# A pair's weighted sums and memory transposes issued as one run of matmuls, with the short pair's last blocks padded to 128 rows

## The chip, the cores and the metric

The kernel runs on one core of a Trainium2 chip. The metric is the device time of one execution in microseconds (us), the median of several runs. Beside those runs stands one execution taken by the hardware profiler, which records every instruction of every engine. The engines are PE (TensorE: matmuls; their weight loads are listed apart as PEld), DVE (VectorE), ACT (ScalarE), POOL (GpSimd) and SP (SyncE, which issues the DMAs). Each engine works through its own queue in order, and semaphores let one engine wait for another.

## The reference: what is computed

Attention over 4 batches, 8 heads, 576 positions and 64 dimensions, mixed with a read of a memory matrix, and then two feed-forward layers over the 2304 tokens:

```python
scores = scale * np.matmul(q, k.transpose(0, 1, 3, 2))      # causal mask, softmax -> a
local = np.matmul(a, v)
q_p = phi(q)                                                # where(x > 0, x, exp(x) - 1) + 1
mem_out = einsum('bhsd,bhde->bhse', q_p, M_prev) / (einsum('bhsd,bhd->bhs', q_p, z_prev)[..., None] + 1e-6)
x = g * mem_out + (1 - g) * local                           # g = sigmoid(beta), one value a head
h = x @ w_in;  x2 = (h * sigmoid(1.702 h)) @ w_out          # 512 -> 2048 -> 512
h = x2 @ w_in2;  out = (h * clip(h + 3, 0, 6) / 6) @ w_out2
```

## The kernel before, in words

**Tiles and pairs.** The tokens are cut into six tiles of 384. Tiles 0, 1, 3 and 4 are the first 384 positions of one batch; tiles 2 and 5 hold the last 192 positions of two batches each. Attention works on pairs of heads: a *long pair* has 384 query rows and 384 keys, a *short pair* has 192 query rows (positions 384 to 575) and 576 keys. There are 16 long pairs, four to each of tiles 0, 1, 3 and 4, and 16 short ones, eight to each of tiles 2 and 5.

**Feed-forward.** For each of two layers and six tiles, 16 units follow one another (`moe`, line 271). A unit makes `h` in four quarters of three matmuls (lines 305 to 307), passes it through a gate (ACT, DVE, ACT, POOL: lines 257 to 268), and adds to four `y` with twelve matmuls (lines 285 to 287). Weights and activations are split into a high and a low part, hence three matmuls where one would stand. The weights arrive raw and are converted by a chain of seven or eight instructions a piece (`conv_w`, lines 188 to 230, on DVE, POOL and ACT), 32 pieces a layer.

**Attention of the next tile runs between the feed-forward matmuls of this one.** The attention of tile 0 is a prologue with no feed-forward beside it. For a pair, `scores` makes the scores `s` and their softmax `p`; `turn` transposes `p` on PE into PSUM (`t`, `t4a`, `t4b`), and ACT or DVE copies it to SBUF (`pt`, and `t4` for the short pair's last 64 keys by 64 rows); `mem_read` (line 626) multiplies phi(q) with the memory (`mem`), and DVE divides and weighs it (`mw`, `mo`, lines 646 to 653); `weigh` (line 663) adds into one PSUM bank `o` the weighted sums `v.T pt`, for the two heads in the two column halves of the array (64 output rows each), and then the transposes of `mo` through the identity. ACT copies `o` to `x`, and `split_x` (line 247) makes of `x` the `xs` that the next tile's `h` reads.

**Sizes on the array.** The profile writes a matmul's rows*columns of the array: `128*128` for feed-forward, transposes, most scores and the memory read, `128*64` for the weighted sums, `64*64` for the `t4` block and the short pair's last scores, `64*128` for the scores of pairs read unsplit. An fp32 matmul shows as two instructions.

**What sets the order.** The generators yield, and `pump` (line 800) interleaves their pieces with the feed-forward by a rate (PG0, PG1). A scheduler that plans with a model of the engines' times then fixes each engine's order, with two restraints: a feed-forward `h` quarter is issued only after the attention matmul recorded `SLACK` pieces earlier (`behind`, line 303), and named DMAs and weight steps stay in program order. `need` (line 363) only makes sure that the instructions of a chain have been written before their reader is; it is no wait on the chip.

**After the last attention.** The pool of the attention's tiles is closed and its memory given to `x2p`, in which the first six raw pieces of the second layer's weights and the second layer's first activations are loaded. These loads therefore stand behind the last pair's last matmul, and the second layer's conversions behind the loads.

Of the kernel before, what the change touches and what calls it, by code (L numbers as in the profile page):

```python
# [24 lines left out]
KQ = 100  # L25
CR = 3.75
OFF = 3
# [9 lines left out]
T4B = 1  # L37
# [73 lines left out]
def attention_moe_kernel(ctx: ExitStack, tc: tile.TileContext, qk0, sk0, sk1, vm0, vm1, bb, w1, w2, out):  # L111
# [76 lines left out]
    def conv_w():  # L188

        key = layer, f, a = w_jobs[w_at[1]]  # L190
# [160 lines left out]

    def at_transpose(*args):
        on_pe[:] = [PE.transpose(*args).ins]  # L353

    def attention(ap):
        qk, vm, pp, pt, phi, mo, raw, sp = {}, {}, {}, {}, {}, {}, {}, {}
        gens = {}
        norms, cut = [0, 0], set()

# [184 lines left out]
        def evac(jobs):  # L544

            yield
            for e, out, in_ in jobs:
                if e is ACT:
                    ACT.copy(out=out, in_=in_)
                else:  # L550
                    DVE.tensor_copy(out=out, in_=in_)

        def turn(i):
            ti, si, b, g, p, _ = pairs[i]
            if g == 0:
                pt[i] = []
                for a in range(2):
# [4 lines left out]
                    for jj in range(2):  # L562
# [4 lines left out]
                        start(("t", i, a, jj), evac([((ACT, DVE)[EV0[jj]], t[:, jj * 384:(jj + 1) * 384], ps[:, 0:384])]))  # L567
                        yield
            else:
                t4 = ap.tile([64, 2, 64], F32, tag="t4", bufs=T4B, name="t4")  # L570
                pt[i] = []
                for a in range(2):
# [4 lines left out]
                    for j in range(4):  # L577
# [3 lines left out]
                        evac([((ACT, DVE)[EV1[a]], t[:, :, 0:128], ps.rearrange("p (j c) -> p j c", j=4))]),  # L581
                    )
                    yield
                pt[i].append(t4)
# [3 lines left out]
                for j in range(3):  # L588
# [8 lines left out]
                        [((ACT, DVE)[EV1[2 + a]], pt[i][a][:, 0:3, 128:192], v[:, :, a]) for a in range(2)]  # L597
                        + [(DVE, pt[i][a][:, 3, 128:192], ps2[:, a * 64:(a + 1) * 64]) for a in range(2)]
                        + [(DVE, t4, ps2[0:64, 128:256].rearrange("p (a c) -> p a c", a=2))]
# [5 lines left out]
        def rows(g):  # L605
            return ((0, 128), (128, 128), (256, 128)) if g == 0 else ((0, 128), (128, 64))
# [19 lines left out]
        def mem_read(i):  # L626
# [7 lines left out]
            for k, (r0, nr) in enumerate(rr):  # L634
                at_matmul(a[0:nr, k * 130:(k + 1) * 130], lhsT=e[:, r0:r0 + nr], rhs=m, start=True, stop=True)
# [4 lines left out]
            def scale():  # L640
                yield
                v = a[:, 0:390].rearrange("p (k c) -> p k c", k=3)
                grp = ((0, 3, 128),) if g == 0 else ((0, 1, 128), (1, 2, 64))
                for k0, k1, nr in grp:
                    wk = w[0:nr, k0:k1]
                    DVE.tensor_scalar(out=wk, in0=v[0:nr, k0:k1, 128:130], scalar1=1e-6, scalar2=None, op0=ALU.add)
                    DVE.reciprocal(out=wk, in_=wk)
                    DVE.tensor_tensor(
                        out=wk, in0=wk, in1=gall[0:nr, None, 2 * p:2 * p + 2].to_broadcast([nr, k1 - k0, 2]), op=ALU.mult
# [277 lines left out]
```

## Time and profile before

| | us |
|---|---|
| median of 3 runs (1100.32 to 1103.64) | 1102.02 |
| the profiled execution's own time | 1097.73 |
| its span, first to last instruction | 1095.9 |
| PE busy in the span | 1052.0 (96%) |
| DVE, ACT, POOL busy | 570.7, 539.1, 472.1 |

The granted clock is the part of TensorE's full rate (2.4 GHz) that it got in a stretch; its lower level is half (1.2 GHz). "Busy" counts an instruction from its start to its modelled end, so for PE the distance from one start to the next is the better price. An engine's idle time costs only where something later waits for it, and the stretches of this kernel differ in which engine that is.

### The profile page before, as it was taken

The numbers are of one execution on the slowest core, as the hardware profiler recorded it, in microseconds if no ns is written. First come the engines' busy times: TensorE is split into PE (matmuls) and PEld (weight loads), VectorE is DVE, ScalarE is ACT, GpSimd is POOL, SyncE is SP. The second block draws the span as 40 slices with busy tenths as digits, with TensorE's granted clock in tenths as the row PEclk, the third lists the DMA queues.
The fourth block names the chain that finished last, engine by engine and source line by source line (L and its number), as shares of the span: only waits on it lengthen the run. The fifth ranks groups of instructions, "written<-read, shape, count | busy, mean of one in ns | idle before, by whom it ended". The sixth has DMA issues, their size and how long they took to land.

```text
span 1095.9 us, 17060 instructions
## 1 busy us (share of the span) xinstructions
PE 1052.0 (96%) x6153; PEld 958.1 (87%) x6153; DVE 570.7 (52%) x1511; ACT 539.1 (49%) x1225; POOL 472.1 (43%) x526
## 2 busy tenths in 40 slices
PE   7988779999999999999999998998999999999998
PEld 5566667788889999889888997998999999999998
DVE  7899999635766564435445588884111121111210
ACT  6766665544555555435443566765233232332422
POOL 5688867544444435444543344543222222222221
PEclk9989989999999999999999998999999999999999
DMA  7542322212231212212120585101000010000000
GB/s 245 202 184 101 121 82 63 73 58 74 82 106 54 63 40 82 69 48 73 44 63 25 204 294 176 57 1 44 15 29 30 1 59 1 30 29 1 30 1 29
DMA packets 32627, 81.77 MB, mean 75 GB/s; under 512 B 3744, under 2 KB 12960, under 8 KB 32544
## 3 DMA queue, kind: packets, MB, share of 16 engines
q1 hardware_dynamic: 32544, 80.69, 21.9%
q8 instruction: 48, 0.79, 0.3%
q14 instruction: 35, 0.29, 0.1%
HBM read 71.24 MB, written 9.44 MB: 74 GB/s over the span
## 4 chain that ended last, share of the span: by engine, by line
PE 76%; DVE 11%; issue 6%; POOL 5%; ACT 1%; DMA 1%; SPq 0%; POOLq 0%; ACTq 0%; DVEq 0%
PE h L305 10%; PE h L307 10%; PE h L306 10%; PE y L287 10%; PE y L286 10%; PE y L285 10%; PE o L350 6%; PE s L350 5%; PE t L353 3%; POOL r L209 2%; POOL g L268 2%; DVE r L205 2%; DVE r L200 2%; PE mem L350 1%; DVE s L391 1%
## 5 line engine op out<-in xcount | busy, mean ns | idle before, releaser
L268 POOL TENSOR_TENSOR g<-t,g 128x384 fp32r<-128x384 f32 x176 | 183.5, 1043 | 407.7 <-ACT g L266 380.9
L305 PE MATMUL h<-xs,w 128*128 128x384 f32 x768 | 266.9, 348 | 19.8 <-DVE t L259 12.3
L306 PE MATMUL h<-xs,w 128*128 128x384 f32 x768 | 261.1, 340 | 0.3 <-DVE w L228 0.3
L307 PE MATMUL h<-xs,w 128*128 128x384 f32 x768 | 261.1, 340 | 0.3 <-DVE xs L251 0.2
L285 PE MATMUL y<-g,w 128*128 128x384 f32 x768 | 259.1, 338 | 0.6 <-ACT g L266 0.5
L286 PE MATMUL y<-g,w 128*128 128x384 f32 x768 | 257.4, 336 | 0.0
L287 PE MATMUL y<-g,w 128*128 128x384 f32 x768 | 241.4, 339 | 3.1 <-DVE g L268 2.9
L263 DVE SCALAR_TENSOR_TENSOR t<-t,h 128x384 f32<-128x384 f32 x96 | 53.1, 553 | 272.1 <-ACT t L261 272.1
L305 PEld LDWEIGHTS h<-xs,w 128*128 128x128 f32 x768 | 147.2, 192 | 30.3 <-DVE t L259 16.7
L266 ACT CAST g<-t 128x384 fp32r<-128x384 f32 x192 | 98.5, 513 | 111.6 <-DVE t L259 56.8
L287 PEld LDWEIGHTS y<-g,w 128*128 128x128 f32 x768 | 141.4, 188 | 9.1 <-DVE g L268 3.9
L307 PEld LDWEIGHTS h<-xs,w 128*128 128x128 f32 x768 | 146.8, 191 | 1.6 <-DVE xs L251 1.1
L306 PEld LDWEIGHTS h<-xs,w 128*128 128x128 f32 x768 | 147.2, 192 | 1.1 <-DVE w L228 0.6
L285 PEld LDWEIGHTS y<-g,w 128*128 128x128 f32 x768 | 144.7, 188 | 3.2 <-issue 1.0
L286 PEld LDWEIGHTS y<-g,w 128*128 128x128 f32 x768 | 144.5, 188 | 0.3
L261 ACT ACTIVATE t<-h,three 128x384 f32<-128x384 f32 x96 | 55.6, 579 | 169.6 <-PE h L307 169.6
L404 POOL TENSOR_SCALAR p<-p,st,omg 128x128 f32<-128x128 f32 (+2 forms) x128 | 93.4, 737 | 84.3 <-DVE st L400 58.7
L391 DVE CUSTOM_DVE_ANT_0 s<-s,mask 128x128 f32<-128x128 f32 (+2 forms) x144 | 73.8, 519 | 74.7 <-PE s L350 73.5
L396 ACT ACTIVATE p<-s,st 128x128 f32<-128x128 f32 (+3 forms) x160 | 82.9, 524 | 25.7 <-DVE st L391 23.3
L259 DVE SCALAR_TENSOR_TENSOR t<-t,h 128x384 f32<-128x384 f32 x96 | 52.7, 549 | 62.1 <-ACT t L257 59.0
L257 ACT ACTIVATE t<-h 128x384 f32<-128x384 f32 x96 | 47.0, 490 | 61.6 <-PE h L307 54.4
L209 POOL TENSOR_SCALAR r<-r 128x512 f32<-128x512 f32 x64 | 57.1, 895 | 30.5 <-DVE r L205 22.4
(86 smaller groups left out, 1348.2 us busy)
## 6 DMA issues: line engine op xcount, KB each, us to landing
r<-in_w_dram SPq DMA_DIRECT2D x64, 512.0 KB, 5.0
raw<-in_sk_dram SPq DMA_DIRECT2D x50, 384.0 KB, 3.2
vm<-in_vm_dram SPq DMA_DIRECT2D x16, 386.0 KB, 3.0
x2d<-yo SPq DMA_DIRECT2D x24, 192.0 KB, 2.0
xr<-x2d SPq DMA_DIRECT2D x24, 192.0 KB, 3.1
out_dram<-yo SPq DMA_DIRECT2D x24, 192.0 KB, 1.9
vm<-in_vm_dram SPq DMA_DIRECT2D x16, 258.0 KB, 2.8
qk<-in_qk_dram SPq DMA_DIRECT2D x7, 384.0 KB, 3.8
```

The costliest lines, as they stand in the source:

```text
L266: gated["ACT"].append(ACT.copy(out=g[:, 0], in_=t).ins)
L268: d = (DVE, POOL)[GLE[ti if layer == 0 else -1]].tensor_tensor(out=g[:, 1], in0=t, in1=f32(g[:, 0]), op=ALU.subtract)
L285: PE.matmul(ys[d], lhsT=w[:, 0, o:o + 128], rhs=g[:, 0], start=(f == 0), stop=False)
L286: PE.matmul(ys[d], lhsT=w[:, 1, o:o + 128], rhs=g[:, 0], start=False, stop=False)
L287: PE.matmul(ys[d], lhsT=w[:, 0, o:o + 128], rhs=g[:, 1], start=False, stop=(f == NF - 1))
L305: PE.matmul(h, lhsT=w[:, 0, c:c + 128], rhs=x[:, 0], start=(kk == 0), stop=False)
L306: PE.matmul(h, lhsT=w[:, 1, c:c + 128], rhs=x[:, 0], start=False, stop=False)
L307: PE.matmul(h, lhsT=w[:, 0, c:c + 128], rhs=x[:, 1], start=False, stop=(kk == KD - 1))
L350: on_pe[:] = [PE.matmul(out, **args).ins]
L391: DVE.tensor_tensor_reduce(out=o, in0=o, in1=m, scale=-SCALE, scalar=init, op0=ALU.add, op1=ALU.min, accum_out=out)
L396: ACT.activation(out=dst, in_=o, func=AF.Exp, scale=-1.0, bias=m, accum_out=s)
L404: (DVE, POOL)[e[norms[0] % len(e)]].tensor_scalar(out=dst, in0=dst, scalar1=s, scalar2=w, op0=ALU.mult, op1=ALU.mult)
```

## The change

Five things are edited. `weigh` first asks for everything that the pair needs, and issues its weighted sums and memory transposes through `in_a_run`: the first matmul waits for the last copy of `pt`/`t4` and the last `mo` on each engine, and the others are chained to it in order, with no yield between them. For short pairs, the `t4` block becomes one tile of 128 rows whose lower 64 rows are zero, set once. The memory read's second block takes rows 64 to 191 instead of 128 to 191, so that it too has 128 columns; the gates `gall` grow to four slices, the last of them zero for the 64 rows that are there twice, so one group of small DVE instructions serves both blocks and the second memory transpose is 128 by 128. A weight piece is started only when the piece four before it has been written out in full. The rates follow the smaller number of yields: KQ 100 to 90, 48 to 44, 76 to 67.

```diff
-KQ = 100
+KQ = 90
...
-T4B = 1
+GW = (0, 2)
...
     def conv_w():
 
-        key = layer, f, a = w_jobs[w_at[1]]
+        n = w_at[1]
+        key = layer, f, a = w_jobs[n]
+        if n >= 4 and w_jobs[n - 4] in w_gen:
+            chains.finish(w_gen[w_jobs[n - 4]])
...
+    def after(ins, deps):
+
+        for dep in deps:
+            tc.add_manual_dep(
+                ins, dep.name, mybir.DependencyInfo(mybir.DependencyClass.Sync, mybir.DependencyReason.DATA),
+                reason="one run of matmuls",
+            )
+
+    def in_a_run(deps):
+
+        run = []
+
+        def mm(out, **args):
+            ins = PE.matmul(out, **args).ins
+            if run:
+                tc.add_manual_dep(
+                    ins, run[-1].name,
+                    mybir.DependencyInfo(mybir.DependencyClass.NoSync, mybir.DependencyReason.DATA),
+                    reason="one run of matmuls",
+                )
+            else:
+                after(ins, deps)
+            run.append(ins)
+            on_pe[:] = [ins]
+
+        return mm
...
+        t4 = ap.tile([128, 2, 64], F32, tag="t4", bufs=1, name="t4")
+        POOL.memset(t4, 0.0)
...
-                        + [(DVE, t4, ps2[0:64, 128:256].rearrange("p (a c) -> p a c", a=2))]
+                        + [(DVE, t4[0:64], ps2[0:64, 128:256].rearrange("p (a c) -> p a c", a=2))]
...
-            return ((0, 128), (128, 128), (256, 128)) if g == 0 else ((0, 128), (128, 64))
+            return (0, 128, 256) if g == 0 else (0, N1 - 128)
...
-            for k, (r0, nr) in enumerate(rr):
-                at_matmul(a[0:nr, k * 130:(k + 1) * 130], lhsT=e[:, r0:r0 + nr], rhs=m, start=True, stop=True)
+            nb = len(rr)
+            for k, r0 in enumerate(rr):
+                at_matmul(a[:, k * 130:(k + 1) * 130], lhsT=e[:, r0:r0 + 128], rhs=m, start=True, stop=True)
...
+                DVE.tensor_tensor(out=wk, in0=wk, in1=gall[:, GW[g]:GW[g] + nb, 2 * p:2 * p + 2], op=ALU.mult)
...
+            need(("t", i, 0, 0), ("t", i, 0, 1), ("t", i, 1, 0), ("t", i, 1, 1), ("m", i))
             o = bank("o")
+            mm = in_a_run(list(made.pop(i).values()))
...
             if g == 0:
-                need(("t", i, 0, 0), ("t", i, 1, 0))
-                av(0, lambda a: t[a][:, 0:384], 0, 384, 128, True)
-                yield
-                need(("t", i, 0, 1), ("t", i, 1, 1))
-                av(1, lambda a: t[a][:, 384:640], 128, 384, 128, False)
-                av(2, lambda a: t[a][:, 640:768], 256, 384, 128, False)
+                av(0, lambda a: t[a][:, 0:384], 0, 384, True)
+                av(1, lambda a: t[a][:, 384:640], 128, 384, False)
+                av(2, lambda a: t[a][:, 640:768], 256, 384, False)
             else:
-                need(("t", i, 0, 0), ("t", i, 1, 0), ("t", i, 0, 1))
                 for j in range(4):
-                    av(j, lambda a: t[a][:, j], 0, N1, 128, j == 0)
-                    if j == 1:
-                        yield
-                av(4, lambda a: t[2][:, a], 128, N1, 64, False)
-            need(("m", i))
+                    av(j, lambda a: t[a][:, j], 0, N1, j == 0)
+                av(4, lambda a: t4[:, a], 128, N1, False)
...
+            POOL.memset(gall[0:64, 3], 0.0)
+            ACT.copy(out=gall[:, 1:3], in_=gall[:, 0:1].to_broadcast([128, 2, H]))
+            ACT.copy(out=gall[64:128, 3], in_=gall[64:128, 0])
...
-                pump((qi - OFF) / (PG0 * 128 / 48 if TILES[ti + 1][0][1] == 0 else PG1 * 128 / 76))
+                pump((qi - OFF) / (PG0 * 128 / 44 if TILES[ti + 1][0][1] == 0 else PG1 * 128 / 67))
```

The order of PE's instructions in the prologue, around the weighted sums of the third pair (a long one); `o<-pt,vm` are the weighted sums, `o<-ident,mo` the memory transposes, `t` the transposes of `p`, `s_...` the scores. First before:

```order
L353 MATMUL t<-ident,p 128x128 x5
L350 MATMUL o<-pt,vm 64x384
L350 MATMUL s_496<-qk 128x128
L350 MATMUL s_496<-qk 128x256
L350 MATMUL s_516<-qk 128x384
L353 MATMUL t<-ident,p 128x128 x3
L350 MATMUL s_546<-qk 128x128
L350 MATMUL s_546<-qk 128x256
L350 MATMUL o<-pt,vm 64x384
L353 MATMUL t<-ident,p 128x128 x3
L350 MATMUL o<-pt,vm 64x256
L353 MATMUL t<-ident,p 128x128 x2
```

The order of PE at the same place of the change, the third pair's weighted sums again:

```order
L353 MATMUL s_501<-qk 128x128
L353 MATMUL s_501<-qk 128x256
L383 MATMUL t<-ident,p 128x128 x6
L368 MATMUL o<-pt,vm 64x384 x2
L368 MATMUL o<-pt,vm 64x256 x2
L368 MATMUL o<-pt,vm 64x128 x2
L368 MATMUL o<-ident,mo 128x128 x3
L353 MATMUL s_571<-qk 128x384
```

What stood in four pieces, one head's matmul apart from the other's, stands in one.

PE's order in the feed-forward of tile 4, around a short pair of tile 5 (`o<-t_...` is the `t4` block); before:

```order
L287 MATMUL y_5424<-g,w_931 128x384
L350 MATMUL o<-pt,vm 64x192 x4
L350 MATMUL s_5932<-sp 128x512 x2
L350 MATMUL o<-pt,vm 64x192 x4
L350 MATMUL o<-t_5742,vm 64x64 x2
L350 MATMUL o<-ident,mo 128x128
L350 MATMUL o<-ident,mo 128x64
L353 MATMUL t<-ident,p 128x128 x4
```

PE's order around a short pair at that place in the change:

```order
L290 MATMUL y_5392<-g,w_1041 128x384
L368 MATMUL o<-pt,vm 64x192 x8
L368 MATMUL o<-t_111,vm 64x64 x2
L368 MATMUL o<-ident,mo 128x128 x2
L353 MATMUL s_5898<-sp 128x512 x2
L383 MATMUL t<-ident,p 128x128 x4
```

The scores have moved behind the run, and both memory transposes have one shape. (The order names a matmul by its output rows and columns of data; the padded `t4` block has the same 64x64 here, on 128 rows of the array.)

The last pair of all on PE, before: the end of its run, and the start of tile 4's last unit (weights `w_1766`; `xs_5275` is tile 4's):

```order
L350 MATMUL o<-t_6353,vm 64x64 x2
L287 MATMUL y_5423<-g,w_1688 128x384
L285 MATMUL y_5424<-g,w_1688 128x384
L286 MATMUL y_5424<-g,w_1688 128x384
L350 MATMUL o<-ident,mo 128x128
L350 MATMUL o<-ident,mo 128x64
L287 MATMUL y_5424<-g,w_1688 128x384
L305 MATMUL h<-xs_5275,w_1766 128x384
```

The last pair of all on PE in the change; `xs_6490`, `xs_6496`, `xs_6502` are the first three quarters of tile 5, and `w_1791` is tile 4's last unit:

```order
L310 MATMUL h<-xs_6502,w_322 128x384
L288 MATMUL y_5389<-g,w_1791 128x384
L289 MATMUL y_5389<-g,w_1791 128x384
L288 MATMUL y_5390<-g,w_1791 128x384
L289 MATMUL y_5390<-g,w_1791 128x384
L288 MATMUL y_5391<-g,w_1791 128x384
L289 MATMUL y_5391<-g,w_1791 128x384
L288 MATMUL y_5392<-g,w_1791 128x384
L289 MATMUL y_5392<-g,w_1791 128x384
L368 MATMUL o<-pt,vm 64x192 x8
L368 MATMUL o<-t_111,vm 64x64 x2
L368 MATMUL o<-ident,mo 128x128 x2
```

Before, the run ends ahead of tile 4's last unit; now it stands behind that unit's 12 `h` and the 12 `y` of the unit before it, nine `h` of tile 5 and eight `y` of the last unit, 41 feed-forward matmuls later.

DVE's order there in the change (`mo` is the last pair's scaled memory, `xs_6508` tile 5's fourth quarter, `t<-t,h` a gate, `r_6537` and `r_6539` the second layer's first raw pieces):

```order
L682 TENSOR_TENSOR mo<-mem,mw 128x128 x2
L254 TENSOR_TENSOR xs_6508<-x_5891,xs_6508 128x384
L262 SCALAR_TENSOR_TENSOR t<-t,h 128x384
L203 TENSOR_SCALAR r_6537<-r_6537 128x512
L262 SCALAR_TENSOR_TENSOR t<-t,h 128x384 x2
L203 TENSOR_SCALAR r_6539<-r_6539 128x512
```

The first conversion stands behind the gate of a tile-5 unit, as it did before, but that gate now needs a quarter which the last run makes.

## Rows read from the trace of the kernel before

**Rows 1.** Five stretches (--windows): length, busy (instructions) by engine, clock, DMA share, GB/s.

```profile
0.00:56.00 56.00, 47.74 (x236) 29.08 (x236) 45.37 (x190) 39.04 (x118) 33.59 (x53) 0.97 0.64 227
56.00:197.00 141.00, 117.67 (x633) 97.85 (x632) 138.83 (x297) 89.81 (x196) 110.41 (x104) 0.92 0.31 106
197.00:611.50 414.50, 414.15 (x2587) 362.43 (x2588) 217.84 (x763) 207.44 (x536) 178.55 (x225) 1.00 0.21 65
611.50:753.20 141.70, 133.28 (x748) 130.22 (x746) 113.26 (x164) 94.98 (x173) 66.99 (x64) 0.98 0.39 134
753.20:1095.90 342.70, 339.19 (x1954) 338.56 (x1954) 55.37 (x101) 107.86 (x205) 82.60 (x82) 1.00 0.07 24
```

**Rows 2.** PE's timeline: a short pair cut by scores; columns start, busy us.

```profile
545.26 0.87 PE L350 MATMUL o<-pt,vm 128*64 128x192 f32 x8
546.06 0.73 PE L350 MATMUL s<-sp 128*128 128x512 f32 x2
546.72 0.87 PE L350 MATMUL o<-pt,vm 128*64 128x192 f32 x8
547.52 0.33 PE L350 MATMUL o<-t,vm 64*64 64x64 f32 x4
547.79 0.53 PE L350 MATMUL o<-ident,mo 128*128 128x128 f32 x2
548.25 0.66 PE L353 MATMUL t<-ident,p 128*128 128x128 f32 x4
```

**Rows 3.** PE's timeline: a short pair's sums not cut.

```profile
592.09 1.52 PE L350 MATMUL o<-pt,vm 128*64 128x192 f32 x16
593.54 0.33 PE L350 MATMUL o<-t,vm 64*64 64x64 f32 x4
```

**Rows 4.** PE's timeline: a memory read of a short and of a long pair.

```profile
251.14 0.75 PE L350 MATMUL mem<-vm,phi 128*128 128x130 f32 x4
251.82 0.73 PE L350 MATMUL s<-sp 128*128 128x512 f32 x2
...
331.40 0.83 PE L350 MATMUL mem<-vm,phi 128*128 128x130 f32 x6
331.99 0.60 PE L287 MATMUL y<-g,w 128*128 128x384 f32 x2
```

**Rows 5.** The chain that ended last, 10 to 70 us: start, us, what.

```profile
16.94 0.79 PE o L350 x2
19.75 0.79 PE o L350 x2
21.38 1.28 PE o L350 x11
...
61.10 1.98 PE o L350 x14
```

**Rows 6.** Waits of DVE, 0 to 56 us: total, times, longest.

```profile
DVE s L391 <- PE s L350: 2.2, 4, 0.9
...
DVE mw L646 <- PE mem L350: 1.5, 2, 1.2
```

**Rows 7.** Groups by form (--lines --by-form): busy us, mean ns.

```profile
L350 PEld LDWEIGHTS mem<-vm,phi 128*128 128x128 f32 x128 | 18.9, 200 | 3.6 <-issue 1.6 <-ACT pt L549 1.3 <-ACT r L215 0.6
...
L350 PEld LDWEIGHTS mem<-vm,phi 128*64 128x64 f32 x32 | 3.1, 134 | 2.0
...
L788 ACT ACTIVATE gall<-gall 128x8 f32<-128x8 f32 x1 | 0.2, 193 | 0.0
```

**Rows 8.** PE's timeline: tile 4's last unit, and the second layer's first matmul.

```profile
607.27 0.34 PE L305 MATMUL h<-xs,w 128*128 128x384 f32 x1
...
679.71 0.69 PE L305 MATMUL h<-xs,w 128*128 128x384 f32 x1 [5.25 <-ACT xs L250]
```

**Rows 9.** SP's and then DVE's timeline: the second layer's first loads and conversion.

```profile
607.20 2.79 SPq L152 DMA_DIRECT2D r<-in_w_dram  x6
...
618.03 0.43 DVE L200 TENSOR_SCALAR r<-r 128x512 int32<-128x512 int32 x1
```

**Rows 10.** DMA issues of the page: count, KB each, us to landing.

```profile
r<-in_w_dram SPq DMA_DIRECT2D x64, 512.0 KB, 5.0
```

**Rows 11.** Waits of PE, 56 to 197 us: total, times, longest.

```profile
PE h L305 <- DVE t L259: 11.0, 5, 4.3
...
PE o L350 <- ACT pt L549: 1.0, 1, 1.0
```

More of the change, by code (lines that the diff above doesn't have):

```diff
@@ L548, in evac @@
                 if e is ACT:
-                    ACT.copy(out=out, in_=in_)
+                    d = ACT.copy(out=out, in_=in_)
                 else:
-                    DVE.tensor_copy(out=out, in_=in_)
+                    d = DVE.tensor_copy(out=out, in_=in_)
+                made.setdefault(i, {})[e] = d.ins
         def turn(i):
@@ L566, in turn @@
                             at_transpose(ps[:, x * 128:(x + 1) * 128], s[y][:, c:c + 128], ident)
-                        start(("t", i, a, jj), evac([((ACT, DVE)[EV0[jj]], t[:, jj * 384:(jj + 1) * 384], ps[:, 0:384])]))
+                        start(("t", i, a, jj), evac(i, [((ACT, DVE)[EV0[jj]], t[:, jj * 384:(jj + 1) * 384], ps[:, 0:384])]))
                         yield
             else:
-                t4 = ap.tile([64, 2, 64], F32, tag="t4", bufs=T4B, name="t4")
                 pt[i] = []
@@ L596, in turn @@
                     evac(
-                        [((ACT, DVE)[EV1[2 + a]], pt[i][a][:, 0:3, 128:192], v[:, :, a]) for a in range(2)]
+                        i, [((ACT, DVE)[EV1[2 + a]], pt[i][a][:, 0:3, 128:192], v[:, :, a]) for a in range(2)]
                         + [(DVE, pt[i][a][:, 3, 128:192], ps2[:, a * 64:(a + 1) * 64]) for a in range(2)]
-                        + [(DVE, t4, ps2[0:64, 128:256].rearrange("p (a c) -> p a c", a=2))]
+                        + [(DVE, t4[0:64], ps2[0:64, 128:256].rearrange("p (a c) -> p a c", a=2))]
                     ),
@@ L641, in scale @@
                 yield
[L642 to L649, printed above, removed]
-                    )
-                yield
-                for k, (r0, nr) in enumerate(rr):
-                    DVE.tensor_tensor(
-                        out=o[0:nr, k * 128:(k + 1) * 128].rearrange("p (a d) -> p a d", a=2),
-                        in0=v[0:nr, k, 0:128].rearrange("p (a d) -> p a d", a=2),
-                        in1=w[0:nr, k, :, None].to_broadcast([nr, 2, D]),
+                v = a[:, 0:nb * 130].rearrange("p (k c) -> p k c", k=nb)
+                wk = w[:, 0:nb]
+                DVE.tensor_scalar(out=wk, in0=v[:, :, 128:130], scalar1=1e-6, scalar2=None, op0=ALU.add)
+                DVE.reciprocal(out=wk, in_=wk)
+                DVE.tensor_tensor(out=wk, in0=wk, in1=gall[:, GW[g]:GW[g] + nb, 2 * p:2 * p + 2], op=ALU.mult)
+                yield
+                for k in range(nb):
+                    d = DVE.tensor_tensor(
+                        out=o[:, k * 128:(k + 1) * 128].rearrange("p (a d) -> p a d", a=2),
+                        in0=v[:, k, 0:128].rearrange("p (a d) -> p a d", a=2),
+                        in1=w[:, k, :, None].to_broadcast([128, 2, D]),
                         op=ALU.mult,
                     )
+                made.setdefault(i, {})[DVE] = d.ins
             start(("m", i), scale())
```

32 lines of the change are left out of this document (15 added, 17 removed).

## The prediction, written before the changed kernel ran

> **What bounds the kernel now.** I read the windows first, because 96% busy PE is a mean over stretches with different limits [rows 1]. From 197 to 611.5 us (tiles 1 to 4 of the first layer with the attention of tiles 2 to 5) PE is busy 414.15 of 414.5 us, DVE about half: here every matmul taken out shortens the run by its own distance to the next start. From 56 to 197 us DVE is busy 138.83 of 141 and PE only 117.67: DVE's conversions set the pace and PE's savings are worth nothing. In the prologue, to 56 us, neither is full, but DVE waits for PE in it, 2.2 us for scores and 1.5 for memory reads [rows 6]. From 611.5 to 753.2 the second layer's conversions run beside tile 5, and PE loses 8.4 us, 5.25 of them in one wait at 679.71 for ACT's `xs`, which stands in ACT's queue among conversions [rows 8]. The last 342.7 us are feed-forward alone, 1954 matmuls in 339.19 us: 0.174 us a matmul, which I use as their price. Then I read PE's timeline around attention, since only the starts show what a matmul costs in its place [rows 2 to 4].
>
> **What a change of size costs.** The cut short pair: eight instructions of the weighted sums take 0.80 us to the next start (545.26 to 546.06), the other eight 0.80 (546.72 to 547.52), together 1.60; sixteen uncut take 1.45 [rows 2, 3]. The scores between the halves take 0.66; at the feed-forward's rate (384 columns in 0.174) their two instructions of 512 columns would take 0.46, an estimate from rows 1. A cut thus costs 0.15 + 0.20 = 0.35 us: leaving and re-entering the array's halves, and the overlap of one head's last matmul with the other's.
>
> The Trainium skill says why ("TensorEngine Tiling (Array Packing)", Key Properties): changing the tiling mode, not just the tile, drains TensorE. It gives no price; the rows above agree and give it.
>
> **The change, part by part.**
>
> *Padding, 197 to 611.5 us.* A short pair's memory read takes 0.68 us for four instructions, two of them 64 columns wide; the long pair's takes 0.59 for six of full width, so four would take 0.39 [rows 4]: 0.29 less at best, and 0 at worst if the neighbours' sizes made the difference. The two memory transposes take 0.46 (547.79 to 548.25) [rows 2]; at the full-width read's 0.10 an instruction, which have about as many columns, two take 0.20: 0.26 less at best; I take 0.15, since their weights are fresh each time. The `t4` block takes 0.27 for four instructions [rows 2]; at the rate of the uncut sums (1.45/16 for 192 columns) four of 64 take 0.12, so 0.15 less at best, 0.10 taken. Together 0.55 a pair (0.70 to 0.25). Padding adds rows and columns that ride in the same time. Of the 16 short pairs two run before 197 us, where it is worth nothing: 14 x 0.55 = 7.7 us.
>
> Here one rule speaks against the change. The memory read's weight load takes 200 ns with 128 columns and 134 with 64 [rows 7]. The Trainium skill ("TensorE: Matmul & The Clock Gate", LDWEIGHTS) says that a weight load's time goes with its columns and not with its rows; the durations agree in direction. If those loads stood on the path, 32 of them would give back 32 x 66 ns = 2.1 us. The starts of rows 4 say that they don't: the mode with the longer loads is the faster one per instruction.
>
> *One run.* In PE's order between the first `h` of tile 1 and the first of tile 5, 22 pairs' sums and transposes stand in 51 pieces before and 28 now. Without the padding's own, 38 changes of size fewer remain, two to a cut: 19 cuts of 0.35 = 6.6 us (2.9 if only 0.15 of a cut is real). In the prologue a long pair's sums are worse cut, head from head: 0.79 + 0.79 + 1.28 = 2.86 us [rows 5], while 14 of the 15 instructions uncut take 1.98, so some 2.1 for all. The order shows all four pairs uncut now: 3.0 us of PE's time. It reaches the end only where DVE waited for PE, 3.7 us in all [rows 6]; I take half, 1.5, between 3.0 and a loss of 4 (next point).
>
> *The wait added.* The run's head waits for the last copies and the last `mo`; behind it in PE's queue stand scores and transposes of the next pairs and feed-forward. Where PE is the bound, ACT and DVE are half idle, and the order puts feed-forward between; I cost it at nothing there. In the prologue PE has little else to do; one wait of 1 us (as the one that rows 11 show, for ACT's `pt`) at each of four heads would cost 4.
>
> *The late end of attention.* The last run now stands 41 feed-forward matmuls later in PE's order, 41 x 0.174 = 7.1 us. The second layer's first weights are loaded as soon as that run ends (607.20) and first converted at 618.03 [rows 9]. With 14.3 + 1.5 saved ahead of it, the last run ends at 607.2 - 15.8 + 7.1 = 598.5. Then come 25 feed-forward matmuls (4.4 us), the fourth quarter's three and the gate, about 6 us, before DVE reaches the first raw piece; the load's 5.0 us [rows 10] fit under that. Conversions start at 604.5, 13.5 us earlier than before, while PE's stream is 15.8 earlier. The wait at 679.71 is set by the conversions, so it grows by 2.3, from 5.25 to about 7.5 us. I let the conversions decide.
>
> *The rest.* The new constraint on weight pieces and the rates move no conversion out of its stretch: up to the first quarter of tile 1, DVE has the same conversions in its order before and now. One memset and two copies of the gates, of the size of their exponential (0.193 us [rows 7]), stand at the very start; were nothing to hide them, they would cost some 0.6. A short pair's six small steps on DVE (`mw`) become three, almost all of them where DVE is half idle.
>
> Sum: 7.7 + 6.6 + 1.5 - 2.3 = 13.5. The profiled execution took 1097.73 us (span 1095.9), so 1084.2 in its terms. The median of the runs stands 4.3 above it at 1102.02: 1088.5.
>
> **The rivals.**
>
> *Conversions start late.* If the first six loads land late, or DVE's order holds the first conversion longer, the second layer's stream starts only some 6 us earlier, and the rest of the gain turns into the wait of rows 8 (some 13 us long): 1096. For: the six loads are issued together and share the DMA engines. Against: a load takes 5.0 us at the median. Chance 0.14.
>
> *Heads block the stretch that DVE bounds (slower).* Ten runs stand before 197 us, four in the prologue and six in tile 0. There `mo` queues on DVE behind conversions; if each head holds PE for 2 us, the feed-forward's `h` and so the gates come late, and DVE, which works in order, stops in front of the gate: PE waited 11.0 us for gates there as it is [rows 11], and DVE has only 2.2 us of slack [rows 1]. Ten heads of 2 us cost 20 against 15 gained: 1107. It decides above 1.5 us a head. Against: the order puts other pairs' work between the memory read and the head. Chance 0.08.
>
> *The run is no run.* The chain fixes only the order inside it; in seven of the 32 pairs the order still has other work inside. If cuts cost nothing where PE has other work at hand, and padding only what its columns cost, nothing remains: 1102. Rows 2 and 3 speak against it. Chance 0.07.
>
> *Weight loads on the path.* If the wider blocks' loads (200 against 134 ns, 32 of them [rows 7]) can't be hidden, 2.1 us are given back: 1090.6. Chance 0.05. The Trainium skill's rule on weight loads, cited above, would have it so.
>
> **How the numbers follow.** The forecast, 1088.5, has 0.66. Its own range: padding 3.5 to 9.8, cuts 2.9 to 6.6, prologue -4 to +3.0, the late end 0 to -2.3, of which the ends seldom meet: 1082 to 1096. Toward the slow side the first rival is taken in, and 2 us each way for the spread of the runs' median: 1081 to 1098. A change under 0.3% (3.3 us) can't be told from none here. Faster: 0.66 + 0.05 + most of 0.14 = 0.84; the same: 0.08; slower: 0.08.
>
> **What would show it.** Right: tile 5's first `h` near 594 us instead of 611.5; a short pair's run of 16, 4 and 2 instructions in some 1.9 us between its neighbours' starts; memory reads of four at 0.45; PE still without waits from tile 1 to tile 5; the first conversion of the second layer near 604.5, and the wait before the second layer at 7 us or more. Wrong: waits of PE for `mo` or `pt` at the head of a run, above all before 190 us; tile 1 starting later than 197; the second layer's first conversion after 612; cut pairs that cost no more than uncut ones.

## The result, and the profile after

The change takes 1086.25 us (1085.44 to 1088.22) beside 1101.17 for the kernel before on the same chip: 14.9 us less by the medians and 13.6 by the ratio of 0.9876 [0.9856, 0.9896], against 13.5 foretold (1102.02 to 1088.5). The total came out as forecast. Its parts did not: tiles 1 to 4 gained more than forecast, the prologue nothing, and one edit that I had priced at zero (the rates) costs some 4 us. Two of the executions below, one of e5 (1670.54 us) and the profiled one of e9 (1284.91 us), ran at a mean granted clock of 0.56 and 0.75 and are used in no comparison, so e9 has a time but no stages.

The profiled execution of the change took 1085.44 us. These are its windows, the stretches of [rows 1] again (length, busy by engine with instructions, clock, DMA share, GB/s):

```profile
0.00:56.80 56.80, 46.31 (x238) 30.56 (x239) 47.52 (x193) 40.42 (x122) 36.98 (x58) 0.89 0.68 245
56.80:199.00 142.20, 117.47 (x639) 95.98 (x639) 134.19 (x290) 90.65 (x199) 110.92 (x102) 0.92 0.29 97
199.00:594.60 395.60, 394.20 (x2556) 360.47 (x2557) 212.79 (x717) 204.73 (x531) 180.80 (x226) 1.00 0.21 65
594.60:739.40 144.80, 136.58 (x771) 132.87 (x769) 112.61 (x166) 95.37 (x174) 68.21 (x64) 0.96 0.39 139
739.40:1083.70 344.30, 340.73 (x1954) 340.09 (x1954) 55.32 (x101) 107.97 (x205) 82.53 (x82) 1.00 0.07 24
```

Read down the lengths. Tiles 1 to 4 fell from 414.5 to 395.6 us; all the others grew: prologue 0.8, tile 0 1.2, the fourth stretch 3.1, the last 1.6 (not in the change's other profile, e3 below: from the second layer's tile 1 on it takes 342.8 us, as before; the last section shows the difference). In tile 0, DVE's idle time rose from 2.2 to 8.0 us although its work shrank by 4.6.

PE's timeline of a short pair in the change (start, busy us), and a memory read of four, to hold against [rows 2 to 4]:

```profile
255.03 1.52 PE L368 MATMUL o<-pt,vm 128*64 128x192 f32 x16
256.38 0.28 PE L368 MATMUL o<-t,vm 128*64 128x64 f32 x4
256.60 0.44 PE L368 MATMUL o<-ident,mo 128*128 128x128 f32 x2
256.79 0.71 PE L353 MATMUL s<-sp 128*128 128x512 f32 x2
...
267.72 0.61 PE L353 MATMUL mem<-vm,phi 128*128 128x130 f32 x4
268.08 0.42 PE L308 MATMUL h<-xs,w 128*128 128x384 f32 x1
```

From start to start the run takes 1.76 us: 1.35, 0.22 and 0.19. Before, cut, it took 1.60 + 0.27 + 0.46 = 2.33 beside the scores [rows 2]. The uncut sums cost 1.35, not the 1.45 of [rows 3]: there the last of the sixteen was followed by a block of another size, here by one of the same. The transposes fell from 0.46 to 0.19.

What was late next, from PE's waits in tile 0 of the change (total, times, longest), its two largest:

```profile
PE h L308 <- DVE t L262: 8.7, 9, 1.6
PE o L368 <- DVE mo L682: 3.5, 1, 3.5
```

PE's waits in tiles 1 to 4 of the change, the only row:

```profile
PE h L308 <- DVE t L262: 1.3, 2, 0.9
```

One head of a run waits 3.5 us for `mo` in tile 0, and none after it: in tiles 1 to 4 PE is without a wait of note. At the end of attention, from PE, SP and DVE of the change, to hold against [rows 8, 9]:

```profile
666.65 0.69 PE L308 MATMUL h<-xs,w 128*128 128x384 f32 x1 [3.28 <-ACT xs L253]
...
599.81 2.79 SPq L152 DMA_DIRECT2D r<-in_w_dram  x6
...
605.97 0.42 DVE L203 TENSOR_SCALAR r<-r 128x512 int32<-128x512 int32 x1
```

The first conversion starts at 605.97 (604.5 foretold) and the second layer at 666.65, 13.06 us earlier than before, though tile 5 starts 16.83 earlier (611.45 to 594.62).

### The profile page after: what moved, and what is told of

Same layout as the page of the kernel before. It is cut to its first block, busy times and chain, and to the rows that moved or that the text cites. A ratio compares the mean times of both kernels' runs of the same rounds, so it can differ in the third digit from the quotient of the medians.

```text
span 1083.7 us, 17025 instructions
## 1 busy us (share of the span) xinstructions
PE 1035.3 (96%) x6153; PEld 960.0 (89%) x6153; DVE 562.4 (52%) x1463; ACT 539.1 (50%) x1227; POOL 479.4 (44%) x528
## 5 line engine op out<-in xcount | busy, mean ns | idle before, releaser
L271 POOL TENSOR_TENSOR g<-t,g 128x384 fp32r<-128x384 f32 x176 | 186.7, 1061 | 428.9 <-ACT g L269 408.4
L437 POOL TENSOR_SCALAR p<-p,st,omg 128x128 f32<-128x128 f32 (+2 forms) x128 | 98.2, 775 | 59.5 <-DVE st L433 37.5
```

Of the source, the lines that this page charges most:

```text
L271: d = (DVE, POOL)[GLE[ti if layer == 0 else -1]].tensor_tensor(out=g[:, 1], in0=t, in1=f32(g[:, 0]), op=ALU.subtract)
L437: (DVE, POOL)[e[norms[0] % len(e)]].tensor_scalar(out=dst, in0=dst, scalar1=s, scalar2=w, op0=ALU.mult, op1=ALU.mult)
```

## The experiments

Each is compared with the kernel before on its own chip (1097.76 us for the first four, 1099.55 for the next four, 1099.17 for the last). The stages are read from the first `h` of a tile (T0 to T5 of the first layer, T6 and T7 the first two of the second); T1 to T5 is tiles 1 to 4. Times of two chips differ by a few us, so kernels of different chips are held together by their ratios.

| kernel | us | ratio | T0 | T1 | T1 to T5 | T5 | T5 to T6 | T6 to T7 |
|---|---|---|---|---|---|---|---|---|
| before (profile) | 1101.17 | 1 | 55.94 | 197.00 | 414.5 | 611.45 | 68.3 | 73.4 |
| change (profile) | 1086.25 | 0.9876 [0.9856, 0.9896] | 56.83 | 198.96 | 395.7 | 594.62 | 72.0 | 72.7 |
| e3 change again | 1085.03 | 0.9878 [0.9865, 0.9891] | 55.86 | 199.36 | 395.6 | 595.01 | 72.0 | 72.7 |
| e1 padding only | 1091.82 | 0.9940 [0.9928, 0.9952] | 55.28 | 199.71 | 404.1 | 603.82 | 68.3 | 73.4 |
| e2 run only | 1098.19 | 0.9992 [0.9981, 1.0002] | 56.54 | 199.14 | 405.8 | 604.96 | 72.5 | 72.7 |
| e4 SLACK 6 | 1088.88 | 0.9915 [0.9899, 0.9930] | 57.02 | 202.42 | 399.2 | 601.62 | 68.2 | 73.4 |
| e5 last run early | 1085.89 | 0.9879 [0.9864, 0.9894] | 55.95 | 200.30 | 398.0 | 598.31 | 68.3 | 73.4 |
| e6 KQ 100 | 1081.10 | 0.9837 [0.9823, 0.9850] | 52.32 | 189.59 | 400.8 | 590.40 | 72.0 | 72.7 |
| e7 runs from the 11th pair | 1083.84 | 0.9860 [0.9845, 0.9876] | 57.00 | 194.13 | 398.3 | 592.41 | 72.6 | 72.7 |
| e8 transposes not padded | 1090.18 | 0.9926 [0.9911, 0.9940] | 57.32 | 199.46 | 398.9 | 598.40 | 72.3 | 72.7 |
| e9 before, KQ 90 | 1106.95 | 1.0065 [1.0052, 1.0079] | | | | | | |
| e10 KQ 110 | 1087.11 | 0.9891 [0.9878, 0.9905] | 51.17 | 200.06 | 395.7 | 595.79 | 72.6 | 72.9 |
| e11 KQ 100, last run early | 1080.38 | 0.9835 [0.9822, 0.9849] | 53.20 | 190.91 | 403.1 | 594.06 | 68.3 | 73.3 |
| e12 `t4` not padded | 1087.76 | 0.9898 [0.9885, 0.9912] | 55.74 | 199.81 | 397.3 | 597.07 | 72.2 | 72.7 |

**Padding alone, run alone.** Padding alone keeps the old pieces in `weigh` and the old rates:

```diff
-KQ = 90
+KQ = 100
...
-            need(("t", i, 0, 0), ("t", i, 0, 1), ("t", i, 1, 0), ("t", i, 1, 1), ("m", i))
...
-            mm = in_a_run(list(made.pop(i).values()))
+            mm = at_matmul
...
```

> Padding alone, the weighted sums issued in pieces as before, with the rates of before. If time goes with changes of size on PE: tiles 1 to 4 shorter by 14 x 0.55 = 7.7 us (3.5 to 9.8), prologue and tile 0 as before within 1 us, the last pair's run ahead of tile 4's last unit, so nothing lost at the second layer's start: 7.7 us faster in all. Rival (the gain of the change comes from the new order and rates, not from sizes): under 3 us.

Run alone keeps the change's `weigh` and rates and undoes the padding:

```diff
-            return (0, 128, 256) if g == 0 else (0, N1 - 128)
+            return ((0, 128), (128, 128), (256, 128)) if g == 0 else ((0, 128), (128, 64))
...
-                av(4, lambda a: t4[:, a], 128, N1, False)
+                av(4, lambda a: t[2][:, a], 128, N1, False, 64)
```

> The run alone, with the rates that belong to it; blocks of the short pair unpadded. If a cut costs 0.35 us: tiles 1 to 4 shorter by 19 x 0.35 = 6.6 us and by some 2.5 that move behind tile 5's start; the late end gives back some 2 us, prologue and tile 0 1 to 2 us longer as in the change: 4 to 6 us faster in all. If only the lost overlap of 0.15 is real: 2.9 less 3, no gain. Rival (order and rates): as much as the whole change, 13 us.

The change itself ran beside them:

> The change itself, on the same chip as the parts, as their measure: 12 to 15 us faster, ratio 0.9856 to 0.9896.

In tiles 1 to 4 the parts nearly add up: 10.3 less with the padding (414.45 to 404.11), 8.6 with the run, 18.8 with both. In the totals they don't: by the ratios 6.6 us less, 0.9 (where 4 to 6 were expected), and 13.4. Each version also starts tile 1 some 2 to 3 us later than before (e1's expectation had at most 1), and the run moves 3.7 us behind T5. A count settles part of that: the kernel before has 867 matmuls ahead of tile 1's first `h`, and all three have 875; eight matmuls have moved, about 1.2 us at 0.15 each (403.56 us of PE's work in e1's stretch over 2578), so 10.3 holds about 9.1 of padding. Without such moved work the run alone gives 5.0 and both together 15.2, about 1 us more than the parts (the sums are in the next section).

**The late end.** The first attempt lowered the tolerance by which attention may fall behind in every tile:

```diff
-SLACK = 10
+SLACK = 6
```

> The change with SLACK 6 in place of 10: a feed-forward quarter may run ahead of attention by fewer pieces. In the order the last pair's run then stands ahead of tile 4's last unit, 43 feed-forward matmuls earlier than in the change, with as many changes of size. If the late end of attention sets the second layer's conversions: the first conversion within 8 us of tile 5's first h (11 in the change), the wait of PE for ACT's xs under 4 us, and 2 us faster than the change. Rival (the wait is set by ACT's order, whenever conversions start): same waits before the second layer, same time as the change within 1 us; and h held back by the smaller slack may cost waits before 197 us.

T5 to T6 went back to 68.2, but the order changed everywhere: tile 1 starts 3 us later and tiles 1 to 4 take 3.6 longer, some 2.4 of it the last run, which stands there again. This run can't price the late end; its one long wait for ACT's `xs` is 5.2 us, not under the 4 that the theory gave. The next one touches only the last tile:

```diff
-            phase["behind"] = lambda: marks[-1 - SLACK] if len(marks) > SLACK else None
+            slack = lambda: 6 if state["emitted"] > 40 and ti == LAST - 1 else SLACK
+            phase["behind"] = lambda: marks[-1 - slack()] if len(marks) > SLACK else None
```

> The change with the last run of the attention moved back from 41 feed-forward matmuls behind the end of tile 4's stream to just ahead of it, by the tolerance of the last tile alone; everything up to tile 3 stands in the same order. Theory (the late end of attention costs the change 1.8 us in the wait before the second layer): tile 1 to tile 5 unchanged at 395.6 plus the 1.9 us of the run that comes back into it, so 397 to 398; tile 5 to tile 6 back from 72.0 to 68.3 us; first conversion of the second layer at most 9 us after tile 5's first h (11.3 in the change); total 1.8 us under the change, near 1083.3. Rival (the wait in front of the second layer is set by how ACT and DVE order the conversions, not by when they begin): tile 5 to tile 6 stays above 70 us and the total is within 0.5 us of the change, 1085.

The theory's stages came true: T1 to T5 398.0, T5 to T6 68.3, the first conversion 6.5 us after T5 (11.3 before the edit). From T1 to T6 it takes 466.3 us, the change 467.7 in both its profiles: 1.4 less, half of which is given back by T7 (539.7 to 540.4, with equal counts of instructions). The total doesn't show it, for tile 0 took 144.4 us here, in the same order of instructions as the change's 142.1 and 143.5. And ACT's `xs` is still waited for, longer: 6.7 us, 5.3 of them in one wait, where the change has 4.8 and 3.3. So most of that wait is not about when the conversions begin; the rival has that part.

**The rate.** One line:

```diff
-KQ = 90
+KQ = 100
```

> The change with the rate KQ of the first conversions put back from 90 to 100, nothing else. Theory (the 4.0 us that PE waits for POOL's p in the prologue come from conversions that the rate of 90 brings earlier, and the 2 us that every version with the run or the padding loses by tile 1 are this): the wait for p falls to about 0.3 us, tile 0 starts 1 to 2 us earlier (near 55), tile 1 near 197, total 1083 to 1084. Rival (tile 1's start is set in tile 0, where DVE and PE wait for one another in turn): tile 1 stays at 199 or later whatever the prologue does, total 1085 or more.

The rate costs time, and more is gained than the theory asked for: 4.8 us less than e5 on the same chip, 4.5 less than the change by the ratios. One clause of the theory fails: e1 had the rate of 100 all along and starts tile 1 at 199.71. What it loses there, some 1.5 us beyond its eight matmuls, is about the spread of tile 0 in one order (last section). Tile 0 starts at 52.32. PE's waits to 56.8 us show one difference (total, times, longest). In the change:

```profile
PE s L353 <- POOL sp L467: 3.7, 1, 3.7
PE t L383 <- POOL p L437: 4.0, 6, 1.2
```

The same waits of PE with KQ 100:

```profile
PE s L353 <- POOL sp L467: 5.3, 2, 5.1
PE s L353 <- ACT p L429: 2.6, 2, 2.0
PE t L383 <- POOL p L437: 0.4, 2, 0.2
```

The short waits of the transposes for POOL's `p` have gone, but new ones for ACT's `p` have come, and the two profiles ran the prologue at different clocks, 0.89 and 0.97. So these rows alone don't show where the 4.5 us between the two T0 come from. e5 has the change's order up to T0 and e11 (below) that of KQ 100, at nearly one clock. The prologue of e5 (PE busy, then clock, DMA share, GB/s), and PE's waits for POOL's `p` in it:

```profile
0.00:55.95 55.95, 44.44 (x238) 0.94 0.71 255
PE t L383 <- POOL p L437: 3.8, 7, 1.2
```

The same of e11:

```profile
0.00:53.20 53.20, 44.98 (x235) 0.92 0.67 238
PE t L383 <- POOL p L437: 0.2, 1, 0.2
```

With 100 tile 0 starts 2.75 us earlier at a clock that is no higher, and PE idles 8.2 us instead of 11.5; so the gain is not the clock's. POOL's timeline (start, busy us) shows what stood before `p`; in the change:

```profile
26.27 1.47 POOL L437 TENSOR_SCALAR p<-p,st,omg 128x384 f32<-128x384 f32 x1
27.71 1.56 POOL L231 TENSOR_TENSOR w<-wtemp,w 128x512 fp32r<-128x512 f32 x1
29.24 0.66 POOL L212 TENSOR_SCALAR r<-r 128x512 f32<-128x512 f32 x1
29.86 2.17 POOL L437 TENSOR_SCALAR p<-p,st,omg 128x128 f32<-128x128 f32 x4
```

POOL's timeline with KQ 100 in the same microseconds:

```profile
26.46 1.26 POOL L231 TENSOR_TENSOR w<-wtemp,w 128x512 fp32r<-128x512 f32 x1
27.71 0.66 POOL L437 TENSOR_SCALAR p<-p,st,omg 128x384 f32<-128x384 f32 x1
29.15 2.02 POOL L437 TENSOR_SCALAR p<-p,st,omg 128x128 f32<-128x128 f32 x3 [0.79 <-ACT pt L582]
```

With 90 two conversion steps of two weight pieces stand one behind the other between two `p` (27.71 to 29.86); with 100 one stands there. DVE begins the first piece at 17.34 with 90 and at 20.95 with 100. The reading is that such a step, which nothing waits for soon, delays what is queued behind it on the same engine; the waits agree, but no run moves these two steps alone. These are the first windows with KQ 100:

```profile
0.00:52.30 52.30, 42.55 (x235) 28.23 (x235) 44.41 (x186) 38.90 (x120) 33.16 (x54) 0.97 0.66 238
52.30:189.60 137.30, 114.88 (x602) 95.23 (x601) 127.93 (x278) 88.15 (x192) 110.47 (x102) 0.91 0.31 109
189.60:590.40 400.80, 398.88 (x2597) 363.43 (x2597) 219.13 (x737) 209.37 (x539) 184.31 (x230) 1.00 0.21 65
```

Ahead of T1 stand 835 matmuls, 40 fewer than in the change, and as many more behind it, so T1 can't be compared; at T5 both have issued the same 3431, and the gain is 594.62 to 590.40, 4.2 us (as from e5 to e11, 598.31 to 594.06).

The same line in the kernel before:

```diff
-KQ = 100
+KQ = 90
```

> The kernel before with one edit of the change alone: KQ 90 instead of 100. Theory (the rate of 90 lets conversions into the engines' queues ahead of attention steps that the first tile needs, whatever the matmuls' order): tile 0 starts 1 to 3 us later than 55.9, total 1 to 4 us over the kernel before, 1099 to 1103. Rival (the rate of 90 costs only together with the run, whose heads wait for the last of everything): total within 1 us of the kernel before, T0 at 56.

7.1 us slower, beyond the theory's range: the rate is bad by itself, and worse without the change's other parts. And the other way:

```diff
-KQ = 90
+KQ = 110
```

> The change with KQ 110, nothing else. Theory (fewer conversions ahead of attention in the prologue is what KQ 100 gained 4 us by, so the start of tile 0 moves on or stays): tile 0 starts at 51 to 53 us, tile 1 at 189 to 195, total 1078 to 1082. Rival (100 is the place at which the orders happen to fit; conversions that come later are missing in tile 0): tile 0 starts early all the same, but tile 0 takes 140 us or more and the total is 1083 to 1086.

The rival's, and slower yet: tile 0 starts earliest of all (51.17), and takes 148.9 us, with DVE busy for 141.3 of them. Against the change, six of DVE's conversion steps have moved from the prologue into tile 0 (24 stand ahead of T0 there, 18 here). Against KQ 100 none has, and only one each of POOL and ACT, so why 110 reaches T5 5.4 us later than 100 is not shown.

**The heads before tile 1.** The head of a run is its first matmul, which waits for all that the run reads. Pairs 1 to 10 in pieces, the rest in runs:

```diff
-            need(("t", i, 0, 0), ("t", i, 0, 1), ("t", i, 1, 0), ("t", i, 1, 1), ("m", i))
+            whole = i >= 10
+            if whole:
+                need(("t", i, 0, 0), ("t", i, 0, 1), ("t", i, 1, 0), ("t", i, 1, 1), ("m", i))
...
-            mm = in_a_run(list(made.pop(i).values()))
+            mm = in_a_run(list(made.pop(i).values())) if whole else at_matmul
...
```

> The change with the run of matmuls only from the eleventh pair on; the first ten pairs (four in the prologue, six in tile 0) have their sums and transposes in pieces again, each piece waiting for its own inputs, as before; padding as in the change. Theory (the heads of the first ten runs cost more in waiting than they save, some 2 us by tile 1): tile 1 starts at 197 to 198 instead of 199.2, tile 1 to tile 5 unchanged within 2 us (395.6), total 1083 to 1084. Rival (the loss by tile 1 is common to padding and run and has nothing to do with the heads): tile 1 at 199 to 200, total 1085 to 1087; the cuts come back in the prologue, and tile 0 starts no earlier than 56.

The heads do cost something in tile 0: it takes 137.1 us and its DVE is busy 134.37 of them, so 2.7 idle where the change has 8.0. Eight matmuls have moved behind T1 with it, and T1 to T5 takes 2.6 longer, more than the "within 2" that the theory gave; at T5, with equal counts (3431 matmuls), 2.2 us are left, and 2.0 of the ratio (whose intervals overlap). The prologue gains nothing without its runs: T0 is 57.00, where e5 and e12, with runs at the same rate and nearly the same clock (0.93, 0.94 and 0.93), have 55.95 and 55.74.

**The paddings one by one.** The second memory transpose on 64 rows again:

```diff
+                if g == 1 and k == 1:
+                    mm(
+                        o[:, 128:192], lhsT=m[64:128, 128:256], rhs=ident[64:128, 64:128], is_transpose=True,
+                        start=False, stop=True, skip_group_check=True,
+                    )
+                    continue
```

> The change with one of its three paddings undone: the short pair's second memory transpose again reads 64 rows (rows 64 to 127 of its tile, the ones that are wanted) and writes 64 columns; the order is the change's. Theory (the transposes' part of the padding is worth 0.15 to 0.26 us a pair, 14 pairs): tile 1 to tile 5 longer by 2.1 to 3.6 us (397.7 to 399.2), total 1087 to 1089. Rival (the padding's 10.4 us lie in the memory reads alone, the one step where a change of size falls among foreign work): tile 1 to tile 5 within 0.7 us of 395.6, total 1085.

The `t4` block on 64 rows again:

```diff
-                    mm(o[h, c0:c1], lhsT=v[:, j, h], rhs=rhs(a), start=first, stop=False, skip_group_check=True)
+                    mm(o[h, c0:c1], lhsT=v[0:kr, j, h], rhs=rhs(a), start=first, stop=False, skip_group_check=True)
...
-                av(4, lambda a: t4[:, a], 128, N1, False)
+                av(4, lambda a: t4[0:64, a], 128, N1, False, 64)
```

> The change with one of its three paddings undone: the short pair's last block of 64 keys is again 64 rows deep (four matmuls on 64 rows, the spare rows of the tile not read); the order is the change's. Theory (that block's part of the padding is worth 0.10 to 0.15 us a pair, 14 pairs): tile 1 to tile 5 longer by 1.4 to 2.1 us (397.0 to 397.7), total 1086 to 1087. Rival (it is worth as much as the transposes, 0.24 a pair, and the three paddings share the 10.4 us of tiles 1 to 4 evenly): 3.3 us longer, total 1088 to 1089.

Both theories hold in tiles 1 to 4: 3.3 us more for the transposes, 1.6 for `t4`. Of the 14 short pairs 13 have their run there (the last run stands behind T5), so that is 0.25 and 0.12 a pair. The whole times rose by more, by 5.3 and 2.2 us by the ratios to e3's. The profile of e8 stands 5.2 us above e3's: 3.3 in tiles 1 to 4, 0.4 elsewhere up to T7, and 1.6 behind T7, where the two ran at different clocks (last section). PE's timeline of the short pair shown above, with the transpose unpadded:

```profile
257.46 0.28 PE L368 MATMUL o<-t,vm 128*64 128x64 f32 x4
257.67 0.53 PE L368 MATMUL o<-ident,mo 128*128 128x128 f32 x2
258.13 0.50 PE L353 MATMUL s<-sp 128*128 128x512 f32 x1
```

PE's timeline of that pair with `t4` unpadded:

```profile
256.01 1.52 PE L368 MATMUL o<-pt,vm 128*64 128x192 f32 x16
257.46 0.33 PE L368 MATMUL o<-t,vm 64*64 64x64 f32 x4
257.72 0.44 PE L368 MATMUL o<-ident,mo 128*128 128x128 f32 x2
```

The transposes take 0.46 to the next start again instead of 0.19. With a smaller `t4`, the sixteen sums ahead of it take 1.45 (256.01 to 257.46) instead of 1.35: the change of size is paid where it happens, in the matmul before it.

**The best of them put together.** KQ 100 and e5's edit:

> The change with KQ 100 and with the last run of the attention ahead of the end of tile 4's stream: the two edits that gained between tiles in the runs before, put together. Theory (the late end costs 1.3 us between tile 1 and tile 6, as the run with the last run moved showed there, and its total missed it only by the scatter of tile 0): tile 1 to tile 6 1.3 us shorter than with KQ 100 alone (472.8), total 1079 to 1080. Rival (what is gained before tile 6 is lost again behind it or in the scatter): total within 0.6 us of 1081.1.

T1 to T6 takes 471.4 us where e6 takes 472.8, so the 1.4 us of e5 come again, and T1 to T7 544.75 where e6 takes 545.53. The totals stand 0.72 apart (1080.38 and 1081.10), which is near the 0.8 left from T1 to T7 but can't be told from nothing: in the profiles e11 reaches T7 0.5 us later than e6, because its tile 1 starts 1.3 later. Both beat the kernel before by 1.6% and the change by about 0.4%.

## Why the prediction was right

The terms of the sum, each with what was measured, up to T7 (753.14 before, 739.34 in the change, 13.8 less):

| term | foretold | measured | by |
|---|---|---|---|
| padding, tiles 1 to 4 | 7.7 | 9.1 | e1, 10.3 less 1.2 of moved work; one by one 14 x (0.30 + 0.25 + 0.12) = 9.4 |
| cuts, tiles 1 to 4 | 6.6 | 6.1 | what remains of the change's 18.8 less padding and moved work |
| prologue and tile 0 | 1.5 | -0.8 | T1 1.96 later, with eight matmuls (1.2) more before it |
| the same at KQ 100 | | +3.4 | e6 at T5, by the same terms |
| late end | -2.3 | -0.7 | T5 to T7; e5 and e11 |
| sum | 13.5 | 13.7 | |

The cuts are what remains, so the sum closes by itself; measured directly, by e2, they are 5.0.

*Padding.* The mechanism is shown: 0.25 a pair for the transposes (e8) and 0.12 for `t4` (e12), against 0.15 and 0.10 taken. The memory read's 0.30 comes from the starts in the trace of e1: 104 matmuls of memory reads in tiles 1 to 4 take 14.8 us to the next start before and 10.7 with padding, 4.2 over 14 pairs; 0.29 was taken. (The three terms taken make 0.54, not the 0.55 that the prediction used.) The step that was mis-sized is "I take 0.15, since their weights are fresh each time": the bound of 0.26 was nearly the price, and fresh weights cost nothing that the starts show.

By the Trainium skill ("TensorE: Matmul & The Clock Gate", LDWEIGHTS) a load's time goes with its columns, which had given me the fourth rival. Tiles 1 to 4 show no price for it: the memory read is the step whose padding widens loads, and in e1 it got 4.2 us shorter. e8 has no bearing on this, since the transposes' loads have 128 columns either way (64x128 or 128x128).

*Cuts.* The change's 18.8 us hold 9.1 of padding, 2.4 of a run that now stands behind T5 (e5 brings it back) and 1.2 for eight matmuls that stand ahead of T1: 6.1 remain for the run. From e2, 8.6 less the same 3.6 leaves 5.0. 6.6 was foretold, from 19 cuts of 0.35. Counted in PE's order between T1 and T5, the size on the array changes 222 times before, 154 times with padding alone, 180 with the run alone and 114 with both. Divided into 9.1, 5.0 and 15.2 us, that is 0.13, 0.12 and 0.14 us for each change that is gone: padding and runs gain at a like price for each change of size, where 0.35 a cut meant 0.175 for each of its two.

The Trainium skill's rule that a change of tiling mode drains TensorE ("TensorEngine Tiling (Array Packing)", Key Properties) agrees with e8 and e12, which put changes of size back and lose 0.25 and 0.12 us a pair.

*The prologue and the rates.* Here the prediction failed, in a step that the total hides. It was "the rates move no conversion out of its stretch: up to the first quarter of tile 1, DVE has the same conversions in its order before and now". The count up to tile 1 is right (116 steps on DVE in both), but it takes the prologue and tile 0 for one stretch: four of those steps, and two each of POOL and ACT, moved from tile 0 into the prologue. Where they stand in a queue was the right question, as on POOL, where two of them stand between two `p`. The rate costs 4.2 us at T5 (e6). (The constraint on weight pieces has no run of its own; e1, which has it at the old rate, issues PE's and DVE's instructions in the old order up to the first padded pair.) With KQ 100 the run gives the prologue 2.1 to 3.0 us, 55.28 in e1 to 53.20 in e11 or 52.32 in e6; 3.0 was what I had worked out as its full worth. With 90 it gives 1.1 to 1.3 (e7 against e5 and e12), and the rate takes that back: tile 0 starts no earlier than the 55.28 of e1. I had halved that term for fear of the heads, and the heads were not what took it: PE waits 0.3 us there for `mo`, and 4.0 for POOL's `p`.

*The heads.* "DVE's conversions set the pace and PE's savings are worth nothing" [rows 1] was also too simple. Once DVE had less to do and the heads held PE, neither engine was full: DVE waited 8.0 us of tile 0. The second rival's mechanism is real at a tenth of its price, about 2 us over ten heads as far as the one run e7 shows, not the 20 that would have turned the sign.

*The late end.* The order of events held (first conversion 1.5 us later than foretold), but the wait did not grow: PE idles 8.2 us in the fourth stretch, 8.4 before, and the longest wait for `xs` fell from 5.25 to 3.28. "I let the conversions decide" failed: e5 brings them forward by 4.9 us against T5 and the wait for `xs` grows.

*The rivals.* Conversions don't start late (605.97, the rival needed some 612). The run is a run: e2's tiles 1 to 4 show it, though its total shows no gain, because the rate takes 7.1 us (e9) of what the run gives. Measured at one KQ each, the run is worth 8.0 us at 90 (1.0065 to 0.9992) and, with padding, 11.3 at 100 (0.9940 to 0.9837); both hold the other two rates too, and the first the constraint on weight pieces. Without e9, e2 would read as "the run is worth nothing". Two of the stated signs of being wrong came true all the same: tile 1 starts later than 197 (198.96), and one head waits 3.5 us for `mo` in tile 0; and the wait before the second layer, said to be 7 us or more, is 3.28.

So the forecast was right partly by errors of opposite sign: 1.4 us too little for padding and 1.6 too much for the late end, against 2.3 too much for the prologue with tile 0 and 0.5 for the cuts.

*What stays open.* How the runs in tile 0 behave at KQ 100 (e7 was run at 90 alone), why 110 is worse than 100, and why ACT's `xs` holds PE for 5 us even when conversions begin early.

## What to carry to other kernels

Price a matmul by the distance to the next start, and where neighbours on the array differ in size, ask first what making them alike would cost: padding rows that ride along were worth 0.65 us a pair here. A rate or a table that "only follows" an edit is an edit: price it by where its instructions land in the queue of the engine that somebody waits for, not by how many there are in a stretch, and undo it alone. Compare stages at points where equal counts of instructions have been issued.

## What was not expected of the hardware

The same order of instructions ran at two clocks in the prologue. PE's timeline of the third pair's run in the change (start, busy us):

```profile
30.54 2.83 PE L368 MATMUL o<-pt,vm 128*64 128x384 f32 x12 [0.26 <-DVE mo L682]
33.30 0.79 PE L368 MATMUL o<-ident,mo 128*128 128x128 f32 x3
```

The window around it in that kernel (the clock is the third number from the end):

```profile
30.00:34.00 4.00, 3.74 (x17) 1.95 (x17) 3.89 (x18) 3.05 (x10) 3.31 (x6) 0.57 0.01 2
```

PE's timeline of the same run in e5, which has the same instructions up to there:

```profile
30.61 1.52 PE L368 MATMUL o<-pt,vm 128*64 128x384 f32 x12 [0.26 <-DVE mo L682]
32.06 0.55 PE L368 MATMUL o<-ident,mo 128*128 128x128 f32 x3
```

And the window around it there:

```profile
30.00:34.00 4.00, 3.74 (x31) 2.62 (x29) 3.96 (x21) 3.72 (x12) 3.31 (x6) 1.00 0.01 2
```

At 0.57, near the lower level of 1.2 GHz, twelve sums take 2.83 us; at 1.00 they take 1.52. PE had been busy 9.30 of the 10 us before in the one and 9.38 in the other, so what it did just before doesn't tell them apart. T0 is 56.83 in the first and 55.95 in the second. For the same order, T1 came at 198.96, 199.36 and 200.30 us: in tile 0 a difference under 1.5 us between two profiles says nothing.

The second layer's tile 1 has the same. Its first 6 us in the change (PE alone; the clock is again third from the end):

```profile
739.34:745.34 6.00, 5.88 (x23) 0.72 0.44 132
```

And in e3, the same kernel:

```profile
739.73:745.73 6.00, 5.87 (x32) 1.00 0.45 135
```

Just before, PE waits 1.48 us for `xs` in both. Of the thirteen profiles used here nine ran these 6 us at 0.72 to 0.74 and took 68.1 to 68.7 us from T7 to the next tile; four (before, e3, e11, e12) ran them at 1.00 and took 67.1. The edits don't sort them, so 1.0 to 1.6 us in a whole profiled time says nothing of an edit: compare such profiles up to T7.
